# One store per output tile and buffer places taken in turn: a fused linear attention and channel mix on one core

## The chip, the cores and the metric

The kernel runs on one core of one Trainium2 chip. The metric is the time of one execution in microseconds (us) on the device, the median of several runs. A profiled execution gives a trace beside it; its span runs from the first to the last instruction.

## What is computed

The reference has two parts. For batch 8, 8 heads, 576 positions and head size 64, a linear attention:

```python
def phi(x):
    proj = np.einsum('bhsd,df->bhsf', x, w_phi)                 # 64 -> 128
    proj = proj - np.max(np.abs(proj), axis=-1, keepdims=True)
    return np.concatenate([np.exp(proj), np.exp(-proj)], axis=-1)
kv  = np.einsum('bhsf,bhsd->bhfd', phi(k), v)
num = np.einsum('bhsf,bhfd->bhsd', phi(q), kv)
den = np.einsum('bhsf,bhf->bhs', phi(q), phi(k).sum(2))[..., None] + 1e-06
```

The quotient num/den, its heads side by side, is the x of shape (8, 576, 512) of a channel mix, where x_prev is x moved on by one position:

```python
xk = mu_k * x + (1 - mu_k) * x_prev
xr = mu_r * x + (1 - mu_r) * x_prev
k  = np.maximum(xk @ w_k, 0)          # 512 -> 1024
v  = k * k @ w_v                      # 1024 -> 512
out = v / (1 + np.exp(-(xr @ w_r)))   # float32, (8, 576, 512)
```

## The kernel before

The whole program is unrolled. The work is cut into named operations, and the long string `ORDER` gives the order in which they are recorded; each engine executes its own part of that list in order. A name is followed, where it matters, by the engine (`/POOL`), the PSUM place (`:1`) and the number of matmuls that only fill time (`+1@0`). The framework derives the waits between engines from the tiles that an instruction reads and writes. An operation that is meant for the DMA (a name ending in `.d`) records nothing.

*Attention.* There are 32 head pairs, n = 4 x batch + a. Loads bring q and k of a batch to `nat` in bf16 (line 321, GpSimd's queue) and v to `vt` (line 327, SP's or GpSimd's). From batch 2 on, DMA transposes on SP's queue make `qkT` (`tr`, line 352). Each pair is projected (`kp`, `qp`, line 566), VectorE finds the largest magnitudes (`rk`, `rq`, lines 579 and 584), ScalarE takes exponentials (`ea`, `eb`, `qa`, `qb`, lines 605 and 643), TensorE forms `ps_kv` and `ps_nd` (`kv`, `nd`, lines 656 and 677), and VectorE divides into `x_sc` (`ra`, `rd`, lines 685 and 689).

*From attention to mix.* From pair 8 on, a DMA transpose on SP's queue (`xz`, line 700) turns x_sc into `xs`, positions along the free dimension. A small copy (`xu`, line 706) sets the shifted start, `df` (line 726) takes the difference to the position before, and `xa`, `xb` (line 732, VectorE) write `xk` and `xr` for two batches together.

*Channel mix.* A batch has four main tiles of 128 rows x 512, and each two batches share one edge tile of two 64-row halves. `h` (line 810) multiplies by w_k in eight blocks, `rl` (lines 206 and 208) is the relu into `krelu`, `sq` (lines 212 and 214) the square into `kk`; `r` (line 829) and `th` (line 835, tile `rt`) make the gate, `v` (line 843) multiplies by w_v, and `ob` (line 849, VectorE) combines gate and product into the output tile. `so` (line 856) stores it from SP's queue. The edge tile goes the same way (lines 897 to 942). A main tile holds, for two neighbouring values of s, 64 rows p of output position 9p + s, so a 64-row half lies in HBM in rows of 2 KB, 18 KB apart, and the other half begins 2 KB after it. A store is two DMAs of 64 rows, one for each half. The last edge tile is stored in quarters, three on SP's queue and one on ScalarE's.

*Buffers.* SBUF tiles come from pools. A tile name has a number of places (`BUFS`: 4 of `ob`, 3 of `krelu`, 3 of `rt`, 2 of `kk`, 2 of `nat` and so on), and the pool gives out one of them when `tile(...)` is called; the first writer of it waits for the readers of the tile that was there. `krelu`, `rt` and `ob` are called for in the matmul step ahead of the one that writes them:

```python
def vm(ci):
    def f():
        s["v", ci] = ps = motile(("mo", f"v{b}.{ci}"), "ps_v")
        s["o", ci] = mm.tile([128, DM], FP, name="ob", bufs=BUFS["ob"])
```

PSUM has two places "mo" of one bank for h, r, v and the small transposes, and three places "P" of two banks for the attention.

Of the kernel before, what the change touches and what calls it, by code (L numbers as in the profile page):

```python
# [126 lines left out]
so7.2 so7.2.d re3:0 ob7.3 so7.3 so7.3.d ve3.0:1 the3 ve3.1:0 obe3.0 soe3.0.a soe3.0.a.d obe3.1  # L127
soe3.0.b soe3.0.b.d soe3.1.b soe3.1.b.d soe3.1.a soe3.1.a.d
# [32 lines left out]
def kernel(  # L161
# [48 lines left out]
    def square(eng, out_, in_):  # L210
        if eng == "ACT":
            nc.scalar.activation(out_, in_, AF.Square)
        else:
# [4 lines left out]
            "xs": 2, "mhl": 3, "nmq": 3, "nmk": 3, "mT": 3, "kvs": 2, "x": 3, "me": 2, "d": 2, "mTe": 2}  # L218
# [81 lines left out]

    nat, qkT, vt = {}, {}, {}

    def get(dct, key, pool, shape, dtype, name, **kw):
        if key not in dct:
            dct[key] = pool.tile(shape, dtype, name=name, **kw)
        return dct[key]
# [5 lines left out]
    def add_load(b, a0, a1, at, first):  # L312
# [4 lines left out]
        def ld(which):  # L317
            def f():
                t = get(nat, b, inp, [128, NP, 2 * X], BF, "nat")
                src, o = ((k, 0), (q, X))[which]  # L320
                nc.gpsimd.dma_start(out=t[:, a0:a1, o:o + X], in_=heads(src, b, a0, a1))
            return f

        def ldv(c0, c1):
            def f(eng):
                t = get(vt, (b, c0 // 2), inp, [128, 2, X], FP, "vt", bufs=BUFS["vt"])
                (nc.sync if eng == "SP" else nc.gpsimd).dma_start(out=t[:, c0 % 2:c0 % 2 + c1 - c0, :],
                                                                  in_=heads(v, b, c0, c1))
            return f

        def pt(b, a, bk):
            def f():
                i = NP * b + a
                get(qkT, b, inp, [128, NP * R, 128], BF, "qkT")
                ps = motile(("mo", f"pt{i}.{bk}"), "ps_pt")
                st["pb", i, bk] = pb = ps.bitcast(BF).rearrange("p (g t) -> p g t", t=128)
                for g in range(5 * bk, min(R, 5 * bk + 5)):
                    nc.tensor.transpose(pb[:, g - 5 * bk, :], nat[b][:, a, g * 128:(g + 1) * 128], ident)
            return f
# [9 lines left out]
        def tr(p0, p1):  # L349
            def f():  # L350
                t = get(qkT, b, inp, [128, NP * R, 128], BF, "qkT")
                nc.sync.dma_start_transpose(out=t[:, R * p0:R * p1, :],
                                            in_=nat[b][:, p0:p1, :].rearrange("p a x -> p (a x)"))
            return f

        g = 0.95 * n
        if b == 0 and a0 == 0:
            def hk():
                st["kq"] = mm.tile([128, NFC, 512], BF, name="kk").rearrange("p a x -> p (a x)").bitcast(FP)[:, 0:2 * X].rearrange("p (i x) -> p i x", i=2)
                nc.sync.dma_start(out=st["kq"][:, 0, :], in_=heads(k, 0, 0, 1)[:, 0, :])  # L360
# [4 lines left out]
            def ck(i):  # L365
                def f(eng):
                    t = get(nat, b, inp, [128, NP, 2 * X], BF, "nat")
                    o = t[:, 0, i * X:(i + 1) * X]
                    copy(eng, o, st["kq"][:, i, :])
                return f  # L370
# [80 lines left out]
    def add_edge(b, a0, a1, first, it):  # L451
# [5 lines left out]
        def tp():  # L457
            s["ps"] = ps = ptile(A, "ps_e")
            for nm_, dct in (("tk0", tkp), ("tk1", tkn)):
                get(dct, b, mid, [128, NP, 128], BF, nm_)  # L460
# [9 lines left out]
        def rt_():  # L470
            s["m"] = m = small.tile([128, 2, NP], FP, name="me", bufs=BUFS["me"])
# [15 lines left out]
        def mce(eng):  # L487
            s["mT"] = small.tile([128, 128], BF, name="mTe", bufs=BUFS["mTe"])
# [57 lines left out]
    def add_pair(n):  # L546
# [30 lines left out]
        def rk():  # L577
            t = get(cp, "nmk", small, [128, 2, 8], FP, "nmk", bufs=BUFS["nmk"])
# [3 lines left out]
        def rq():  # L582
            t = get(cp, "nmq", small, [128, 2, 8], FP, "nmq", bufs=BUFS["nmq"])
# [18 lines left out]
        def ek(pn):  # L602
            def f():
                s[f"k{pn}"] = mid.tile([128, 8, 128], BF, name=f"k{pn}", bufs=BUFS["kpn"])
# [17 lines left out]
        def mc(eng):  # L622
            cp["mT"] = small.tile([128, 128], BF, name="mT", bufs=BUFS["mT"])
# [15 lines left out]
        def eq(pn):  # L639
            def f():  # L640

                t = s[f"q{pn}"] = mid.tile([128, 8, 128], BF, name=f"q{pn}", bufs=BUFS["qpn"])
# [22 lines left out]
        def kvc(eng):  # L665
            s["kv"] = small.tile([128, 2, 2, 65], BF, name="kv", bufs=BUFS["kvs"])
# [15 lines left out]
        def ra():  # L682
            s["rd"] = small.tile([128, 2, 5], FP, name="rden")
# [3 lines left out]
        def rd():  # L687
            s["x"] = mid.tile([128, 10, 64], BF, name="x_sc", bufs=BUFS["x"])
# [5 lines left out]
        def newx():  # L694
            for dct, nm_ in ((xkt, "xk"), (xrt, "xr")):
                get(dct, bp, mm, [128, NDC, 2 * S], BF, nm_)
# [27 lines left out]
        def df(eng):  # L724
            s["d"] = mid.tile([128, S], BF, name="diff", bufs=BUFS["d"])
# [69 lines left out]
    def add_moe(b):  # L795
# [4 lines left out]
        main = out[b].rearrange("(p s) d -> s p d", s=R)[b % 2:b % 2 + 8]  # L800
        mixa, mixb = ([f"x{i}{4 * b + a}" for a in range(NP)] for i in "ab")

        def h(fc):
            def f():
                s[fc] = ps = motile(("mo", f"h{b}.{fc}"), "ps_h")
                s["kr", fc] = mm.tile([128, 512], BF, name="krelu", bufs=BUFS["krelu"])
                if fc == 0:
                    s["kk"] = mm.tile([128, NFC, 512], BF, name="kk")
# [5 lines left out]
        def rl(fc):  # L814
            def f(eng):
                relu(eng, s["kr", fc], s[fc])
# [7 lines left out]
        def rr(ci):  # L824
            def f():
                s["r", ci] = ps = motile(("mo", f"r{b}.{ci}"), "ps_r")
                s["t", ci] = mm.tile([128, DM], BF, name="rt", bufs=BUFS["rt"])
# [5 lines left out]
        def th(ci):  # L833
            def f():
                nc.scalar.activation(s["t", ci], s["r", ci], AF.Tanh, scale=0.5)  # L835
            return f

        def vm(ci):
            def f():
                s["v", ci] = ps = motile(("mo", f"v{b}.{ci}"), "ps_v")  # L840
                s["o", ci] = mm.tile([128, DM], FP, name="ob", bufs=BUFS["ob"])
# [5 lines left out]
        def ob(ci):  # L847
            def f():
                nc.vector.scalar_tensor_tensor(out=s["o", ci], in0=s["t", ci], scalar=1.0,  # L849
# [3 lines left out]
        def so(ci):  # L853
            def f():
                for i in range(2):
                    nc.sync.dma_start(out=main[2 * ci + i], in_=s["o", ci][64 * i:64 * i + 64, :])
            return f

        for fc in range(NFC):
# [3 lines left out]
               alloc=[("mo", mo), ("krelu", ("krelu", nme))] + ([("kk", ("kk", b))] if fc == 0 else []),  # L863
               rel=[("xk", bp)] if fc == NFC - 1 else [])
            op("rl" + nme, "ACT", 0.6, ("rl",) + t, rl(fc), ["h" + nme], rel=[mo], alt=("ACT", "DVE"))
            op("sq" + nme, "POOL", 1.06, ("sq",) + t, sq(fc), alt=("POOL", "DVE", "ACT"), port=True, deps=["rl" + nme], rel=[("krelu", nme)])
        for ci in range(4):
# [3 lines left out]
               alloc=[("mo", mo), ("rt", ("rt", nme))], rel=[("xk", bp)])  # L871
            op("th" + nme, "ACT", 0.6, ("th",) + t, th(ci), ["r" + nme], rel=[mo])
# [3 lines left out]
               alloc=[("mo", mo), ("ob", ("ob", nme))], rel=[("kk", b)], chain="v")  # L876
            op("ob" + nme, "DVE", 0.7, ("ob",) + t, ob(ci), ["v" + nme, "th" + nme],
# [5 lines left out]
    def add_moe_edge(bp):  # L883
# [4 lines left out]
        def h(half):  # L888
            def f():
                s[half] = ps = motile(("mo", f"he{bp}.{half}"), "ps_he").rearrange("p (i t) -> p i t", i=4)  # L890
                s["kr", half] = mm.tile([128, 512], BF, name="krelu", bufs=BUFS["krelu"])
                if half == 0:
                    s["kk"] = mm.tile([128, NFC, 128], BF, name="kke", bufs=1)
# [9 lines left out]
        def rl(half):  # L903
            def f(eng):
                relu(eng, s["kr", half], s[half].rearrange("p i t -> p (i t)"))
# [7 lines left out]
        def rr():  # L913
            s["r"] = ps = motile(("mo", f"re{bp}"), "ps_re")
            s["t"] = mm.tile([128, DM], BF, name="rt", bufs=BUFS["rt"])
# [4 lines left out]
        def th():  # L920
            nc.scalar.activation(s["t"], s["r"], AF.Tanh, scale=0.5)

        def vm(c0, w):
            def f():
                s["v", c0] = ps = motile(("mo", f"ve{bp}" if w == DM else f"ve{bp}.{c0 // w}"), "ps_ve")
                if c0 == 0:
                    s["o"] = mm.tile([128, DM], FP, name="ob", bufs=BUFS["ob"])
# [5 lines left out]
        def ob(c0, w):  # L933
            def f():
                nc.vector.scalar_tensor_tensor(out=s["o"][:, c0:c0 + w], in0=s["t"][:, c0:c0 + w], scalar=1.0,
# [3 lines left out]
        def so(c0, w, which, e):  # L939
            def f():  # L940
                for i in ((0, 1) if which < 0 else (which,)):
                    (nc.scalar if e == "ACT" else nc.sync).dma_start(
                        out=out[b - 1 + i].rearrange("(p s) d -> s p d", s=R)[8 * (1 - i)][:, c0:c0 + w],
                        in_=s["o"][64 * i:64 * i + 64, c0:c0 + w])
            return f

        for half in range(2):
# [3 lines left out]
               alloc=[("mo", mo), ("krelu", ("krelu", nme))] + ([("kke", ("kke", bp))] if half == 0 else []))  # L951
            op("rl" + nme, "ACT", 0.6, ("rl",) + t, rl(half), ["h" + nme], rel=[mo], alt=("ACT", "DVE"))
# [3 lines left out]
        op("r" + nme, "PE", 0.87, ("un",) + t, rr, mixb + ["wr.d"], chain="r", alloc=[("mo", mo), ("rt", ("rt", nme))],  # L956
           rel=[("xk", bp)])
        op("th" + nme, "ACT", 0.6, ("th",) + t, th, ["r" + nme], rel=[mo])
        t = (4 * b, "ve")
        for hf in range(1 if bp < 3 else 2):  # L960
# [4 lines left out]
               alloc=[("mo", mo)] + ([("ob", ("ob", nme))] if hf == 0 else []), rel=[("kke", bp)], chain="v")  # L965
            op("ob" + nmv, "DVE", 0.7 * w / DM, ("ob",) + t, ob(hf * w, w), ["v" + nmv, "th" + nme],
               rel=[mo, ("rt", nme)])
            for i in ((-1,) if bp < 3 else (0, 1)):
                x = "so" + nmv + ("" if i < 0 else ".a" if i == 0 else ".b")
                e = "ACT" if hf == 1 and i == 1 else "SP"  # L970
                op(x, e, 1.2, ("so",) + t, so(hf * w, w, i, e), ["ob" + nmv])
                op(x + ".d", "DMA", 0.7, ("so",) + t, None, [x], rel=[("ob", nme)])

    BUFS["kke"] = 1
# [42 lines left out]
```

## Time and profile before

| | |
|---|---|
| time, median of 3 runs | 285.87 us |
| lowest and highest run | 284.57 and 334.05 us |
| profiled execution: span from first to last instruction | 275.3 us |
| profiled execution: own time | not given apart from the span; the median of the runs is 10.6 us above it |
| instructions in the trace | 8865 |
| bytes by DMA | 42.89 MB, 156 GB/s over the span |
| HBM read, written | 33.62 MB, 9.44 MB |
| TensorE clock granted | 1.00 |
| stores by SP's queue | 70 of 128 KB and 3 of 64 KB; one of 64 KB by ScalarE's |

Under "busy", PE is TensorE's matmuls and PEld its weight loads, DVE is VectorE, ACT ScalarE, POOL GpSimd and SP SyncE. Registers, semaphores and the issue of DMAs do not count as busy. The chain is followed back from the last instruction, at each step to what released it. The share of a DMA queue is the time of its packets over 16 engines and the span, and "to landing" is the time from the issue of a DMA to its completion.

### The profile page before, as it was taken

What the parts mean: (1) busy time and instruction counts of PE and PEld (TensorE: products, weight loads), DVE (VectorE), ACT (ScalarE), POOL (GpSimd) and SP (SyncE); (2) the same over time, 40 slices, a digit from 0 to 9 for tenths busy, and PEclk for the clock granted to TensorE, in tenths of its full rate; (3) what the DMA queues carried; (4) which work ended last, traced back from release to release, by engine and by line L of the source; (5) the groups of instructions that cost most, each with busy time, mean ns of one, the idle gap of its engine ahead of it and who ended that gap; (6) DMA issues with size and microseconds to landing.
All of it is one profiled execution on the core that took longest, in us unless ns stands there. A gap on an engine that the chain in (4) does not pass through costs nothing.

```text
span 275.3 us, 8865 instructions
## 1 busy us (share of the span) xinstructions
PE 261.7 (95%) x3682; PEld 154.1 (56%) x3730; DVE 234.6 (85%) x388; ACT 223.1 (81%) x413; POOL 142.4 (52%) x193
## 2 busy tenths in 40 slices
PE   7899889999899999999999999999999999999993
PEld 3567656566555566555565666555566565444542
DVE  6999999999799989999999889998889897864222
ACT  3899999999899997899898999789987777616330
POOL 5799557976818682633459465821931611300200
PEclk9999999999999999999999999999999999999999
DMA  7999999599999899759699998981725324142134
GB/s 147 285 209 250 209 213 174 114 235 175 238 129 200 202 219 185 155 127 248 99 166 164 215 249 142 171 255 41 161 89 88 77 52 100 42 110 67 29 88 116
DMA packets 65817, 42.89 MB, mean 156 GB/s; under 512 B 47152, under 2 KB 57008, under 8 KB 65776
## 3 DMA queue, kind: packets, MB, share of 16 engines
q1 hardware_dynamic: 54496, 27.54, 49.3%
q0 software_dynamic: 11056, 14.42, 29.1%
q8 instruction: 29, 0.48, 0.8%
q10 hardware_dynamic: 224, 0.36, 0.5%
q14 instruction: 12, 0.10, 0.1%
HBM read 33.62 MB, written 9.44 MB: 156 GB/s over the span
## 4 chain that ended last, share of the span: by engine, by line
PE 75%; DVE 8%; ACT 6%; issue 4%; DMA 3%; POOL 2%; SPq 0%; POOLq 0%; ACTq 0%
PE ps_h L810 19%; PE ps_v L843 17%; PE ps_r L829 9%; PE ps_nd L677 5%; PE ps_kv L656 5%; DMA qkT<-nat 3%; PE ps_he L897 3%; PE ps_ve L929 3%; PE ps_k L566 2%; PE ps_qT L630 2%; PE ps_q L566 2%; PE ps_qT L636 2%; ACT k L605 2%; DVE nmk L579 2%; PE ps_f L292 1%
## 5 line engine op out<-in xcount | busy, mean ns | idle before, releaser
L597 POOL TENSOR_TENSOR v<-vt,v 128x576 bf16<-128x576 f32 x59 | 69.8, 1203 | 33.5 <-ACT v L591 31.1
L605 ACT ACTIVATE k<-ps_k 128x1024 bf16<-128x1024 f32 x64 | 64.8, 1047 | 1.3 <-DVE nmk L579 1.3
L643 ACT ACTIVATE q<-ps_qT 128x1024 bf16<-128x1024 f32 x64 | 63.8, 1054 | 1.8 <-PE ps_qT L636 1.7
L810 PE MATMUL ps_h<-xk,wk_bf 128*128 128x512 bf16 x235 | 60.5, 380 | 1.2
L843 PE MATMUL ps_v<-wv_bf,kk 128*128 128x512 bf16 x244 | 58.2, 379 | 0.6
L579 DVE TENSOR_REDUCE nmk<-ps_k 128x8 f32<-128x1024 f32 x32 | 38.8, 1217 | 1.8 <-PE ps_k L566 1.5
L584 DVE TENSOR_REDUCE nmq<-ps_q 128x8 f32<-128x1024 f32 x32 | 38.3, 1217 | 1.6 <-PE ps_q L566 1.4
L843 PEld LDWEIGHTS <-kk 128*128 128x128 bf16 x256 | 24.1, 98 | 27.3
L810 PEld LDWEIGHTS <-wk_bf 128*128 128x128 bf16 x256 | 22.7, 97 | 25.0 <-issue 0.7
L206 ACT ACTIVATE krelu<-ps_h 128x512 bf16<-128x512 f32 x48 | 28.8, 611 | 9.3 <-PE ps_h L810 9.3
L726 POOL TENSOR_TENSOR diff<-xs 128x576 bf16<-128x576 bf16 x15 | 20.2, 1346 | 28.8 <-ACT xs L706 12.7
L214 POOL TENSOR_TENSOR kk<-krelu 128x512 bf16<-128x512 bf16 x18 | 19.1, 1068 | 30.3 <-ACT krelu L206 26.6
L849 DVE SCALAR_TENSOR_TENSOR ob<-rt,ps_v 128x512 f32<-128x512 bf16 x32 | 21.7, 682 | 14.3 <-PE ps_v L843 12.7
L829 PE MATMUL ps_r<-wr_bf,xr 128*128 128x512 bf16 x116 | 31.1, 380 | 0.7
L835 ACT ACTIVATE rt<-ps_r 128x512 bf16<-128x512 f32 x32 | 19.7, 615 | 8.8 <-PE ps_r L829 8.7
L732 DVE SCALAR_TENSOR_TENSOR xk<-diff,mu_k_t,xs 128x576 bf16<-128x576 bf16 x32 | 26.7, 839 | 0.1
L689 DVE TENSOR_TENSOR x_sc<-ps_nd,rden 128x640 bf16<-128x640 f32 x32 | 26.0, 817 | 0.6
L732 DVE SCALAR_TENSOR_TENSOR xr<-diff,mu_r_t,xs 128x576 bf16<-128x576 bf16 x32 | 25.6, 806 | 0.1
L656 PE MATMUL ps_kv<-v,k 64*128 64x65 bf16 x1024 | 22.4, 190 | 0.5 <-ACT q L643 0.2
L566 PEld LDWEIGHTS <-qkT 64*128 64x128 bf16 x512 | 16.5, 94 | 11.0 <-issue 8.0
L656 PEld LDWEIGHTS <-k 64*128 64x128 bf16 x1024 | 19.3, 94 | 5.7 <-issue 1.8
L677 PE MATMUL ps_nd<-kv,q 128*128 128x65 bf16 x512 | 21.4, 193 | 0.0
(102 smaller groups left out, 414.3 us busy)
## 6 DMA issues: line engine op xcount, KB each, us to landing
out_dram<-ob SPq DMA_DIRECT2D x70, 128.0 KB, 2.5
vt<-in_v_dram SPq DMA_DIRECT2D x11, 576.0 KB, 6.1
nat<-in_k_dram POOLq DMA_DIRECT2D x6, 576.0 KB, 7.8
nat<-in_q_dram POOLq DMA_DIRECT2D x6, 576.0 KB, 8.0
vt<-in_v_dram POOLq DMA_DIRECT2D x4, 576.0 KB, 6.0
wk_bf<-in_moe_w_k_dram POOLq DMA_DIRECT2D x2, 512.0 KB, 11.4
wv_bf<-in_moe_w_v_dram POOLq DMA_DIRECT2D x2, 512.0 KB, 10.6
nat<-in_k_dram POOLq DMA_DIRECT2D x3, 288.0 KB, 6.9
```

Source lines behind the costliest of these rows:

```text
L206: nc.scalar.activation(out_, in_, AF.Relu, scale=HALF)
L579: nc.vector.tensor_reduce(t[:, j, :], s["k"].rearrange("p a (g f) -> p (a g) f", f=128), axis=AX.X, op=ALU.max, apply_absolute_value=True, ...
L584: nc.vector.tensor_reduce(t[:, j, :], s["q"].rearrange("p a (g f) -> p (a g) f", f=128), axis=AX.X, op=ALU.max, apply_absolute_value=True, ...
L597: (nc.vector if eng == "DVE" else nc.gpsimd).tensor_tensor(vb[:, a, pn, :, 0:64], vt[b, a // 2][:, a % 2, :].rearrange("p (s d) -> p s d", ...
L605: nc.scalar.activation(s[f"k{pn}"], s["k"].rearrange("p a (g f) -> p (a g) f", f=128), AF.Exp, scale=(1.0 if pn == 0 else -1.0))
L643: nc.scalar.activation(t.rearrange("f x (a p) -> f x a p", a=2), s["qT"].rearrange("f a (x p) -> f x a p", p=64), AF.Exp, scale=(1.0 if pn ...
L656: nc.tensor.matmul(ps[:, hh, pn * 65:(pn + 1) * 65], lhsT=s[f"k{pn}"][r, c, :], rhs=vb[r, a, pn, 2 * g + par, :], start=(pn == 0 and c == ...
L677: nc.tensor.matmul(ps[:, bk, o * 65:(o + 1) * 65], lhsT=tail if sl < 2 else s[f"q{pn}"][:, 2 * G + h, :], rhs=s["kv"][:, h, pn, :], start= ...
L732: nc.vector.scalar_tensor_tensor(out=t[:, a, (b % 2) * S:(b % 2 + 1) * S], in0=s["d"], scalar=mu[:, a:a + 1], in1=xs[:, a, 0:S], op0=ALU.m ...
L810: nc.tensor.matmul(ps, lhsT=wk_bf[:, c, fc * 128:(fc + 1) * 128], rhs=xkt[bp][:, c, m0:m0 + 512], start=(c == 0), stop=(c == NDC - 1))
L829: nc.tensor.matmul(ps, lhsT=xrt[bp][:, c, m0 + ci * 128:m0 + (ci + 1) * 128], rhs=wr_bf[:, c, :], start=(c == 0), stop=(c == NDC - 1))
L843: nc.tensor.matmul(ps, lhsT=s["kk"][:, fc, ci * 128:(ci + 1) * 128], rhs=wv_bf[:, fc, :], start=(fc == 0), stop=(fc == NFC - 1))
```

## The change

*Stores.* Each output tile is stored by one DMA of 128 rows instead of two of 64. The destination is written as [2, 64, 512]: the two halves outermost, then 64 rows, then 512 numbers; for the edge tiles the same shape is put together from two addresses. The last edge tile is stored as two pieces of 256 columns, the first on SP's queue, the second on ScalarE's. The string `ORDER` changes in its last line alone.

```diff
         main = out[b].rearrange("(p s) d -> s p d", s=R)[b % 2:b % 2 + 8]
+        main = main.rearrange("(c i) p d -> c i p d", i=2)
...
         def so(ci):
             def f():
-                for i in range(2):
-                    nc.sync.dma_start(out=main[2 * ci + i], in_=s["o", ci][64 * i:64 * i + 64, :])
+                nc.sync.dma_start(out=main[ci], in_=s["o", ci])
             return f
...
-        def so(c0, w, which, e):
-            def f():
-                for i in ((0, 1) if which < 0 else (which,)):
-                    (nc.scalar if e == "ACT" else nc.sync).dma_start(
-                        out=out[b - 1 + i].rearrange("(p s) d -> s p d", s=R)[8 * (1 - i)][:, c0:c0 + w],
-                        in_=s["o"][64 * i:64 * i + 64, c0:c0 + w])
+        def so(c0, w, e):
+            def f():
+                rows = out[b - 1:b + 1].rearrange("i (p s) d -> i p s d", s=R)
+                lo, hi = rows[0, :, R - 1, c0:c0 + w], rows[1, :, 0, c0:c0 + w]
+                both = bass.AP(lo.tensor, lo.offset, [[hi.offset - lo.offset, 2]] + [list(x) for x in lo.ap])
+                (nc.scalar if e == "ACT" else nc.sync).dma_start(out=both, in_=s["o"][:, c0:c0 + w])
             return f
```

*Buffers.* Every place of every SBUF ring becomes a tile of its own with one place, and a counter takes the places in turn. The call moves from the matmul step to the step that writes the tile (`krelu` to `rl`, `rt` to `th`, `ob` to `ob`). The number of places of each ring stays.

```diff
+    used = {}
+
+    def slot(kind):
+        i = used[kind] = used.get(kind, -1) + 1
+        return i % BUFS[kind]
+
+    def ring(pool, kind, shape, dtype, name, i=None):
+
+        i = slot(kind) if i is None else i
+        return pool.tile(shape, dtype, name=name, tag=f"{name}.{i}", bufs=1)
+
...
         def vm(ci):
             def f():
                 s["v", ci] = ps = motile(("mo", f"v{b}.{ci}"), "ps_v")
-                s["o", ci] = mm.tile([128, DM], FP, name="ob", bufs=BUFS["ob"])
...
         def ob(ci):
             def f():
+                s["o", ci] = ring(mm, "ob", [128, DM], FP, "ob")
                 nc.vector.scalar_tensor_tensor(out=s["o", ci], in0=s["t", ci], scalar=1.0,
...
         def rl(fc):
             def f(eng):
+                s["kr", fc] = ring(mm, "krelu", [128, 512], BF, "krelu")
                 relu(eng, s["kr", fc], s[fc])
...
         def df(eng):
-            s["d"] = mid.tile([128, S], BF, name="diff", bufs=BUFS["d"])
+            s["d"] = ring(mid, "d", [128, S], BF, "diff")
```

The other tiles (`nat`, `qkT`, `vt`, `tk`, `me`, `mTe`, `nmk`, `nmq`, `k`, `q`, `mT`, `kv`, `rden`, `x_sc`, `xk`, `xr`, `kk`, `kke`) are edited as `diff` is.

## The prediction

> **What bounds the kernel now.** I read the busy table first, then the chain that ended last, then the DMA queues, because the change touches nothing but stores and buffers.
>
> ```profile
> PE 261.7 (95%) x3682; PEld 154.1 (56%) x3730; DVE 234.6 (85%) x388; ACT 223.1 (81%) x413; POOL 142.4 (52%) x193
> ...
> PE 75%; DVE 8%; ACT 6%; issue 4%; DMA 3%; POOL 2%; SPq 0%; POOLq 0%; ACTq 0%
> ```
>
> TensorE is busy 95% of the span and carries 75% of the chain. DMA has 3% of the chain and SyncE's queue 0%: neither the transfers nor their issue sets the end today. The DMA part and the list of issues:
>
> ```profile
> q1 hardware_dynamic: 54496, 27.54, 49.3%
> q0 software_dynamic: 11056, 14.42, 29.1%
> q8 instruction: 29, 0.48, 0.8%
> q10 hardware_dynamic: 224, 0.36, 0.5%
> ...
> out_dram<-ob SPq DMA_DIRECT2D x70, 128.0 KB, 2.5
> ...
> xs<-x_sc SPq DMA_TRANSPOSE x24, 3.2
> ```
>
> The shares are means over 16 engines. They add up to about 80%, so the engines are well loaded while they are loaded evenly. A half tile's store lands in 2.5 us, and the transposes of x_sc (line 700) go down the same SP queue. Two stretches of the trace say what stores meet (columns: stretch, its length, busy time of the five engines, TensorE clock, DMA share, GB/s):
>
> ```profile
> 70.00:239.00 169.00, 166.04 (x2430) 97.88 (x2462) 155.50 (x242) 147.60 (x267) 85.39 (x113) 1.00 0.79 152
> 239.00:275.30 36.30, 31.88 (x176) 15.88 (x176) 13.62 (x26) 11.63 (x22) 3.31 (x3) 1.00 0.37 85
> 266.60:271.80 5.20, 4.44 (x28) 2.53 (x26) 2.22 (x4) 0.60 (x1) 0.00 (x0) 1.00 0.66 151
> ```
>
> The first store is issued at 71 us, the last transpose at 237.9. The DMA view of the first stretch counts 50 half stores, that of the second 20 halves and four quarters. So the middle holds 25 tiles and the tail 11 in bytes. The third row has nothing but stores in flight. One more view, the DMA of 184.5 to 188.2 us, cut in 40 slices:
>
> ```profile
> DMA  9999999999999999998444211111000000100000
> GB/s 423 399 399 418 407 399 371 412 412 385 451 382 404 379 424 401 380 379 313 180 158 158 113 67 66 44 44 44 22 22 22 22 22 22 44 22 22 0 0 0
> ```
>
> Four half stores were issued from 180.9 on, and this is their burst: about 400 GB/s with all 16 engines full, 25 GB/s for one engine. In the third row above it is 151/(16 x 0.66) = 14.3 GB/s per busy engine. These are my two ends for what one engine does with 2 KB rows.
>
> **What the Trainium skill says.** Page "DMA: Bandwidth & Descriptors", section "Why a DMA increments its semaphore by 16 and not by 1": a copy runs on k engines, the largest k up to 16 that divides the slowest dimension above one of both access patterns, as the instruction carries them; on the hardware queues these are the lowest-numbered k, and each posts one completion. The trace of before agrees for even shapes: q10 carries one load of 128 rows and one store of 64 rows, and 224 - 192 leaves 32 completions, 16 for each. Section "Queues, rings and completion order": each engine consumes a queue's descriptors in ring order, and alternates between queues. No run here shows this by itself. Section "Rules for kernel authors" has two rules that pull apart here: use one 128-partition transfer instead of two halves, and keep a dimension below 16 from standing outermost.
>
> **The change, part by part.** *The store.* Before, a half is 64 rows to 64 rows: 16 engines, 4 rows each. After, the SBUF side is 128 rows, but the built instruction writes a destination of 2 x 64 x 512 (edge tiles too; the last two are 2 x 64 x 256). The slowest dimensions are 128 and 2, so k = 2: all 4608 output rows go through two engines. Per tile: 262,144 bytes / 2 / 25 GB/s = 5.24 us on each, at the low rate 9.17 us; before it was 0.66 to 1.15 us on each of sixteen. I take 5.24, since in the third row 16 engines read 64 rows at a time, and in the burst, with two halves in flight together, they were full speed; two engines alone have less reason to disturb each other.
>
> *What else these two engines carry.* 78.7% of the 169 us of the middle (q1 59.7, q0 18.1, instructions 0.9) is 133 us per engine. The 50 halves are 0.41 MB per engine, 16 to 29 us, so 104 to 117 us are loads and transposes. Part of it counts time twice, when two queues are in service (a stretch at 93 us shows a share of 1.10). At 25 GB/s their 19.2 MB would be 48 us per engine, too little for small packets. I take 90, ends 48 and 117.
>
> *Sum, middle.* 25 x 5.24 = 131, plus 90 = 221 us of work for two engines in 169 us: +52 (ends +10 and +79). So they become the bound. What waits: loads and transposes are spread over all engines and land with their slowest share, and in the SP queue they stand behind up to four stores (the ob ring), 21 us. In order, ob's VectorE instruction (line 849) waits for the store four tiles back; behind it stand the reductions of ps_k and ps_q, the x_sc products and the mixes, hence ScalarE's exponentials, and it holds one of the two "mo" PSUM places, hence TensorE. A late x_sc transpose stops xu, diff, mixes and then h and r.
>
> *Dry time.* While VectorE waits for a transpose that stood behind the stores, no new store is made, and the two engines can run dry afterwards. Before does not show it: from 0 to 50 us. I take 10% of 221, 22 us, because compute needs only 169 of the 221 and can refill the ring of four.
>
> *Tail.* 11 x 5.24 = 58 us, 1 us before the first and 2 us for the last to land, 61 in place of 36.3: +24. TensorE's 31.9 us lie inside.
>
> *Issue.* SP loses 37 of 73 stores' issues at 0.59 us, 22 us, worth nothing at a 0% share of the chain. At the very end ACT's store is the last issued, 0.4 us earlier than SP's last was.
>
> *Rings and waits.* TensorE, VectorE and GpSimd keep their order of instructions exactly. ob's 27 or so waits for two halves become waits for one, and VectorE loses 17 semaphore instructions of about 20 ns: 0.3 us. Some two dozen krelu, diff, me and kv writers wait for a neighbouring earlier reader, because places are taken in strict turn and at the writer instead of at the matmul. Each is within one operation (0.4 to 1.1 us), in either direction, and most are already satisfied: between -2 and +2 us, taken as 0.
>
> *Total.* 275.3 + 52 + 22 + 24 = 373 us of span. The profiled execution's own time is known only as this span; the median of 285.87 lies 10.6 above it, and I add that: 384 us.
>
> **The rivals.** *Sixteen engines all the same* (not slower): the engine count follows the SBUF side's 128 rows. Then both halves leave as one burst at the 25 GB/s seen, ob is free some 0.6 us earlier, the end comes 0.4 us earlier, and SP's queue has 22 us less. For it: the page's account of k is the only ground for two engines, and no DMA of before has a short outer dimension. Against: the built destination does. It decides if stores land in about 2.5 us. It gives 285 us; under 280 only if those 0.6 us reached the chain ten times, and VectorE waited for no store before.
>
> *Two engines at the low rate:* 14.3 GB/s. Middle 25 x 9.17 + 90 + 22 = 341 (+172), tail 101 + 3 (+68): 526 us. For it: the tail's stores ran so before, unloaded by others. Against: that was with 64 rows over 16 engines.
>
> *Two engines, but mostly hidden:* loads cost these engines 48 us, and the ring of four covers the middle; +10 and the tail's +24: 320 us. Against: 0.79 of DMA share in the middle.
>
> **How the numbers follow.** Two engines overloaded, 384: 0.82. Sixteen engines: 0.08. Low rate: 0.06. Hidden: 0.04. The likeliest one's own range is 320 (no dry time, loads at 48) to 439 (117 and 50 us dry); I go to 450 for a rate between the two ends. The rest, sixteen engines and the low rate, is 0.14, and a few hundredths of the main case lie outside. About 2% of the time is what a measurement of this kernel tells from no change: slower 0.91, same 0.07, faster 0.02.
>
> **What would show it.** The list of issues must have 35 stores of 256 KB, landing in 7 us alone and 10 to 20 us in the median; at k = 16 under 3. Completions tell k directly: q1 loses 64 rows to ACT's queue and 73 x 16 completions, and gains 36 x 2: 53,336 packets; at k = 16 it is 53,840. q10 then has 274 instead of 288. ob's line must wait for DMA of out_dram, the xu, diff or mix lines for DMA of xs, and TensorE's share must fall to about 70% with unchanged matmul durations. The mean DMA share must fall although two engines are full, since the bytes are the same in a longer span. If the stores land late and the span still stays under 310, the overload reasoning is wrong; if they land in 2.5 us, the engine count is.

## The result, and the profile after

The changed kernel takes 356.64 us (median of 6 runs, 354.22 to 362.11), the kernel before 284.74 us in the same comparison (6 runs, 278.77 to 334.05). The ratio is 1.277, with a 95% interval of 1.265 to 1.289; it leaves out the runs that a disturbance made longer, which the medians, above all that of the kernel before, still contain, so it lies above their quotient of 1.253. The profiled execution took 356.93 us and has a span of 355.1, so 1.8 us lie around the span. Every profiled execution of the experiments showed 1.7 to 1.9 as well.

Busy times, the clock, and the DMA in 40 slices, from the page of the kernel after:

```profile
PE 278.4 (78%) x3682; PEld 161.0 (45%) x3730; DVE 236.3 (67%) x388; ACT 224.2 (63%) x413; POOL 141.0 (40%) x193
...
PEclk9999999999986559999998998999986999999655
DMA  8999989997959849593999699893291893111111
GB/s 151 267 240 210 206 142 199 170 185 116 155 123 100 121 91 131 128 167 38 200 179 73 134 103 149 64 184 114 70 72 51 75 62 61 52 53 51 51 50 41
```

VectorE, ScalarE and GpSimd did the same work as before to within 2 us. The last six slices tell what the stores run at: 50 to 53 GB/s at a DMA share of one tenth (the last slice, in which they end, has 41). The number that the whole prediction hung on stands in the DMA part, together with the chain:

```profile
q1 hardware_dynamic: 53336, 27.47, 60.2%
q0 software_dynamic: 11056, 14.42, 23.6%
q8 instruction: 29, 0.48, 0.7%
q10 hardware_dynamic: 274, 0.43, 0.4%
...
PE 34%; DMA 28%; DVE 13%; issue 8%; POOL 6%; ACT 3%; SPq 1%; DVEq 0%; POOLq 0%; ACTq 0%
DMA xs<-x_sc 10%; PE ps_v L862 9%; DMA out_dram<-ob 9%; PE ps_h L829 8%; DMA vt<-in_v_dram 8%; PE ps_r L848 4%; PE ps_nd L694 3%; POOL v L610 3%; DVE nmq L597 2%; PE ps_kv L673 2%; DVE nmk L592 2%; DVE xk L751 1%; DVE x_sc L706 1%; DVE xr L751 1%; DMA wph_f<-in_w_phi_dram 1%
```

A completion is, as in the prediction, what an engine posts when its share of a DMA is done; it counts as a packet. 53,336 and 274 packets mean two completions for each store; sixteen would have given 53,840 and 288. DMA went from 3% to 28% of the chain and TensorE fell from 75% to 34%. The DMA part is made up of transposes of x_sc, stores and v loads. The waits, longest first (who waited, for what, us in total, times, longest):

```profile
POOL xs L201 <- DMA xs<-x_sc: 29.2, 6, 10.3
...
POOL v L610 <- DMA vt<-in_v_dram: 24.9, 4, 12.3
ACT xs L199 <- DMA xs<-x_sc: 24.3, 3, 17.4
...
DVE ob L869 <- DMA out_dram<-ob: 23.4, 8, 5.9
```

None of these was among the long waits before. Cut at the end of the last transpose's issue, now 294 us instead of 239, the two stretches of the prediction are these (columns as there):

```profile
70.00:294.00 224.00, 183.37 (x2438) 105.04 (x2472) 157.82 (x245) 150.55 (x270) 85.47 (x115) 0.90 0.98 115
294.00:355.10 61.10, 32.95 (x173) 16.34 (x174) 13.86 (x25) 11.12 (x21) 3.31 (x3) 0.81 0.17 51
```

The middle grew from 169 to 224 us, the tail from 36.3 to 61.1. In the slices in which nothing but stores run, two engines at 51 GB/s are 25.5 GB/s each. That no second pair helps can be counted in the trace's packet records: in the tail the 2 KB packets of the stores are in flight two at a time for 44.9 us, three for 4.5 us, and never more, although stores are queued behind each other.

### The profile page after: what moved, and what is told of

The parts are those of the page before. It is cut to its first block, busy times and chain, and to the rows that moved or that the text cites. A ratio compares the mean times of both kernels' runs of the same rounds, so it can differ in the third digit from the quotient of the medians.

```text
span 355.1 us, 8808 instructions
## 1 busy us (share of the span) xinstructions
PE 278.4 (78%) x3682; PEld 161.0 (45%) x3730; DVE 236.3 (67%) x388; ACT 224.2 (63%) x413; POOL 141.0 (40%) x193
## 3 DMA queue, kind: packets, MB, share of 16 engines
q1 hardware_dynamic: 53336, 27.47, 60.2%
q0 software_dynamic: 11056, 14.42, 23.6%
## 4 chain that ended last, share of the span: by engine, by line
PE 34%; DMA 28%; DVE 13%; issue 8%; POOL 6%; ACT 3%; SPq 1%; DVEq 0%; POOLq 0%; ACTq 0%
DMA xs<-x_sc 10%; PE ps_v L862 9%; DMA out_dram<-ob 9%; PE ps_h L829 8%; DMA vt<-in_v_dram 8%; PE ps_r L848 4%; PE ps_nd L694 3%; POOL v L610 3%; DVE nmq L597 2%; PE ps_kv L673 2%; DVE nmk L592 2%; DVE xk L751 1%; DVE x_sc L706 1%; DVE xr L751 1%; DMA wph_f<-in_w_phi_dram 1%
## 5 line engine op out<-in xcount | busy, mean ns | idle before, releaser
L610 POOL TENSOR_TENSOR v<-vt,v 128x576 bf16<-128x576 f32 x59 | 68.6, 1182 | 49.1 <-DMA vt<-in_v_dram 24.9
L862 PE MATMUL ps_v<-wv_bf,kk 128*128 128x512 bf16 x244 | 63.4, 403 | 7.8 <-POOL kk L213 3.7
L869 DVE SCALAR_TENSOR_TENSOR ob<-rt,ps_v 128x512 f32<-128x512 bf16 x32 | 21.8, 684 | 44.5 <-DMA out_dram<-ob 23.4
L862 PEld LDWEIGHTS <-kk 128*128 128x128 bf16 x256 | 25.3, 103 | 37.9 <-issue 9.2
L848 PE MATMUL ps_r<-wr_bf,xr 128*128 128x512 bf16 x116 | 34.4, 411 | 6.0 <-DVE ob L869 3.3
L205 ACT ACTIVATE krelu<-ps_h 128x512 bf16<-128x512 f32 x48 | 28.9, 609 | 12.9 <-PE ps_h L829 10.9
L673 PEld LDWEIGHTS <-k 64*128 64x128 bf16 x1024 | 19.9, 95 | 11.2 <-issue 5.7
L694 PE MATMUL ps_nd<-kv,q 128*128 128x65 bf16 x512 | 23.0, 200 | 0.0
```

The source lines that it names most:

```text
L610: (nc.vector if eng == "DVE" else nc.gpsimd).tensor_tensor(vb[:, a, pn, :, 0:64], vt[b, a // 2][:, a % 2, :].rearrange("p (s d) -> p s d", ...
L673: nc.tensor.matmul(ps[:, hh, pn * 65:(pn + 1) * 65], lhsT=s[f"k{pn}"][r, c, :], rhs=vb[r, a, pn, 2 * g + par, :], start=(pn == 0 and c == ...
L694: nc.tensor.matmul(ps[:, bk, o * 65:(o + 1) * 65], lhsT=tail if sl < 2 else s[f"q{pn}"][:, 2 * G + h, :], rhs=s["kv"][:, h, pn, :], start= ...
L848: nc.tensor.matmul(ps, lhsT=xrt[bp][:, c, m0 + ci * 128:m0 + (ci + 1) * 128], rhs=wr_bf[:, c, :], start=(c == 0), stop=(c == NDC - 1))
L862: nc.tensor.matmul(ps, lhsT=s["kk"][:, fc, ci * 128:(ci + 1) * 128], rhs=wv_bf[:, fc, :], start=(fc == 0), stop=(fc == NFC - 1))
```

## The experiments

All times are medians; "before" beside each is the kernel before on the same chip. Each version gives one profiled span as well, and what a version costs in us is read from spans, beside the 276.1 us of the rings alone.

**The two halves of the change, taken apart.** First the rings alone (the changed kernel, stores cut again):

```diff
-                nc.sync.dma_start(out=main[ci], in_=s["o", ci])
+                for i in range(2):
+                    nc.sync.dma_start(out=main[ci][i], in_=s["o", ci][64 * i:64 * i + 64, :])
```

(and the edge tiles in the same way).

> The changed kernel with every store as two DMAs of 64 rows again, so that only the rings are new. If the two engines of the merged store are the whole cause: 285 us, within 2% of before, half stores landing in about 2.5 us, no wait of ob for a store. If the strict turn of the buffer places has a part in the slowdown: clearly above 290 us, with the missing part up to 72 us in the other run.

Measured: 277.72 us, before 283.37, ratio 0.986 (0.976 to 0.995), span 276.1, half stores landing in 2.4 us. Then the opposite, the kernel before with the one-DMA stores of the change and its own pools:

> The kernel before with one DMA of 2 x 64 rows for each tile, its pools as they were. Two engines: 356 us, as the whole change, 53,336 packets on q1. If the rings had a part: less than the whole change by that part.

Measured: 357.78 us, before 283.37, ratio 1.272 (1.255 to 1.289), and 53,336 packets on q1. The stores are the whole loss. Whether the rings bring a gain was asked once more:

> The version with the new rings and stores in halves once more, in five rounds, beside the kernel before: the first time it was 1.4% faster with an interval that just left out no change. If the strict turn of the places gains: 0.98 to 0.99 again. If that was the scatter of the kernel before: an interval that takes in 1.

Measured: 277.85 us in 22 runs, before 283.13 in 28, ratio 0.997 (0.994 to 1.000). That takes in 1: no gain that this comparison shows. The runs of this version lie between 277.2 and 280.6 us, those of before between 277.0 and 290.6; that the narrower scatter comes from the rings is not shown.

**Does the loss add up as middle plus tail?** The stores before the last x_sc transpose as two halves, the later ones as one DMA, by a condition on the tile (for the edge tiles, `bp >= 2`):

```diff
+                if not (b >= 6 or (b, ci) == (5, 3)):
+                    for i in range(2):
+                        nc.sync.dma_start(out=main[ci][i], in_=s["o", ci][64 * i:64 * i + 64, :])
+                else:
+                    nc.sync.dma_start(out=main[ci], in_=s["o", ci])
```

> The changed kernel; only the stores after the last transpose of x_sc (11 tiles in bytes) are one DMA, the 25 before it are two halves. By the sum of the prediction only the tail grows, from 36 to 61 us: +24, ratio 1.08 to 1.09, with TensorE's share and clock unchanged until 239 us. If a single overloaded stretch were what slows everything: little here, under +10.

Measured: 303.38 us, ratio 1.075 (1.057 to 1.093), span 301.0. With the condition turned round:

> The other way round: the 25 tiles of the middle in one DMA, the last 11 tiles in two halves. If the parts add up: the last transpose of x_sc moves from 238 to about 292 us, and the tail is 36 us again: +54 to +58, ratio 1.19 to 1.20. If the backlog of the middle reaches into the tail: more than that, up to +72.

Measured: 335.66 us, ratio 1.190 (1.179 to 1.201), span 334.8. The stretches of the first and of the second, cut at the last transpose of each:

```profile
70.00:240.20 170.20, 168.25 (x2456) 99.30 (x2491) 157.41 (x246) 149.76 (x269) 87.06 (x115) 1.00 0.77 153
240.20:301.00 60.80, 32.90 (x175) 16.22 (x176) 13.40 (x26) 11.52 (x22) 3.31 (x3) 0.79 0.14 50
```

```profile
70.00:296.40 226.40, 181.60 (x2444) 104.65 (x2476) 157.99 (x246) 150.35 (x269) 85.53 (x115) 0.92 0.99 114
296.40:334.80 38.40, 31.90 (x175) 15.86 (x176) 14.10 (x26) 11.57 (x22) 3.31 (x3) 1.00 0.38 82
```

Over the span of the rings alone (276.1) they cost 24.9 and 58.7 us, together 83.6; the whole change costs 79.0. The parts add up to within 5 us, and the tail is 61 us wherever it is stored by one DMA, with 50 GB/s in it.

**Is it the number of engines, or the one large DMA?** Here main tiles take every second or every fourth column of the batch's 512, so that one DMA of 128 rows has an outermost destination dimension of 4 or 8. The same stride is used for the gate and for the product; edge tiles are stored as halves.

```diff
-        main = main.rearrange("(c i) p d -> c i p d", i=2)
+        main = [main[4 * (ci // 2):4 * (ci // 2 + 1)].rearrange("s (p u) d -> u s p d", u=2)[ci % 2] for ci in range(4)]
...
-                    nc.tensor.matmul(ps, lhsT=s["kk"][:, fc, ci * 128:(ci + 1) * 128],
+                    nc.tensor.matmul(ps, lhsT=s["kk"][:, fc, 256 * (ci // 2) + ci % 2:256 * (ci // 2 + 1):2],
```

> Main tiles take every second column, so that one DMA of 128 rows has a destination of 4 x 32 x 512; edge tiles as two halves. If the engine count follows the outer dimension: 4 engines, a store takes 2.6 us on each, middle 25 x 2.6 + 90 = 155 of 169 us, tail 29 of 36 us: nearly hidden, 280 to 295 us. If it is one DMA instead of two that costs: about 350 us. q1 must count 4 completions for each of the 32 main stores.

> The same with every fourth column: 8 x 16 x 512, 8 engines, 1.3 us on each. If the count follows the outer dimension: fully hidden, as with two halves, 277 to 285 us. If one DMA of 256 KB costs by itself: about 350 us.

Measured: 306.14 us for 4, 281.08 for 8, before 282.75 (277.71 to 288.12). The spans are 306.9 and 277.8 us, which is 30.8 and 1.7 more than with the rings alone. The DMA rows, first of 4, then of 8:

```profile
q1 hardware_dynamic: 53520, 27.47, 55.7%
```

```profile
q1 hardware_dynamic: 53648, 27.47, 50.1%
```

The rings alone had 54,416 packets. With 32 main stores, 54,416 - 32 x (32 - 4) = 53,520, and 54,416 - 32 x (32 - 8) = 53,648: each store has 4 or 8 completions where its two halves had 32. So one DMA of 256 KB is harmless when eight engines carry it; what costs is how few engines it gets. One large DMA and the stride in the matmuls together cost no more than the 1.7 us at 8. At 4 the expected 280 to 295 us were missed.

**Is a short outer dimension needed for it?** Plain rows, no third dimension, four DMAs for a tile:

```diff
-                nc.sync.dma_start(out=main[ci], in_=s["o", ci])
+                for i in range(2):
+                    for r0, r1 in ((0, 62), (62, 64)):
+                        nc.sync.dma_start(out=main[ci][i][r0:r1], in_=s["o", ci][64 * i + r0:64 * i + r1, :])
```

> No outer dimension at all: each half of a main tile is stored as 62 rows and 2 rows, plain shapes, four DMAs for a tile; edge tiles as halves. The largest number up to 16 that divides 62 is 2. If the count is by that rule: two engines again, 330 to 360 us (edge stores on 16 engines give a little back, twice as many issues on SP take a little). If only a short outer dimension is slow: 277 to 290 us.

Measured: 346.97 us, before 282.75. Its q1 has 53,648 packets: 64 pairs of DMAs with 2 + 2 completions in place of 16. The span of 345.5 us is 69.4 above the rings alone; 32 of the 36 tiles go through two engines, and 32/36 of the 79.0 us of the whole change are 70. So a tile costs as much in 62 rows as in 2 x 64, and 2 is the largest number up to 16 that divides 62. A short outer dimension is not needed.

**Capacity of the two engines, or the place behind the stores in one ring?** All stores on ScalarE's queue:

```diff
-                nc.sync.dma_start(out=main[ci], in_=s["o", ci])
+                nc.scalar.dma_start(out=main[ci], in_=s["o", ci])
```

> The changed kernel with all stores issued from ScalarE's queue, so that the x_sc transposes no longer stand behind stores in one ring; still 2 x 64 rows. If the capacity of the two engines is the bound, as the prediction has it: 345 to 370 us, perhaps more since ScalarE now waits for ob. If the place behind the stores in the ring is what costs: the middle's 54 us go to a good part, 305 to 325 us, and x_sc transposes land in about 3 to 6 us.

Measured: 362.24 us, before 282.75. Nothing came back on balance: the last x_sc transpose is issued at 296.8 us, in the changed kernel at 292.4. ScalarE's queue holds only 3% of this run's chain, some 11 us, so what its own waiting may have eaten seems far from the 55 us by which the middle had grown. As far as this run tells, the place in the ring is not the main cost; it is not a clean separation, since ScalarE now waits too (39.0 us for ps_h, 10.9 in the changed kernel). The waits for x_sc transposes fell from 57 to 23 us, and waits for transposes of q and k took their place:

```profile
POOL xs L201 <- DMA xs<-x_sc: 21.6, 3, 13.9
PEld L479 <- DMA qkT<-nat: 21.6, 3, 13.4
```

**Why four engines cost about 30 us.** (The 23 us in the expectation below is the difference of the two medians; the spans give 30.8.) The chain of that run, transfers alone (start, us, what):

```profile
96.19 23.32 DMA xs<-x_sc
...
169.65 15.51 DMA xs<-x_sc
```

The kernel before, cut finer than in the prediction (three of its stretches):

```profile
70.00:110.00 40.00, 38.31 (x653) 23.71 (x661) 37.35 (x58) 36.01 (x63) 24.25 (x36) 1.00 1.10 195
...
135.00:175.00 40.00, 39.52 (x630) 24.09 (x633) 37.34 (x55) 36.22 (x67) 27.85 (x31) 1.00 1.00 177
...
205.00:239.00 34.00, 33.74 (x445) 19.70 (x447) 30.35 (x53) 25.24 (x45) 8.82 (x11) 1.00 0.35 70
```

The middle is not one bucket. Until 110 us and again from 135 to 175 us the DMA share is 1.10 and 1.00, with 12 and 10 half stores in it, so the other transfers alone nearly fill the engines; late in the middle all of it together needs a third. Both long waits begin within these two stretches. So the first two batches were given their halves back, and four engines kept from batch 2 on:

> Four engines again, but the eight main tiles of the first two batches (stored up to about 130 us) go out as two halves with the columns of before. Why four engines cost 23 us although their work over the whole middle fits: if it is the stretch from 70 to 110 us, where the other transfers alone already fill the engines (share 1.10 before), the stall at 96 to 120 us goes and 288 to 296 us are left, with the second stall, at about 155 to 170 us, still there. If the cost of four engines lies evenly over all tiles: 300 us.

Measured: 288.92 us, before 283.13, ratio 1.032 (1.014 to 1.049). The span is 287.1, 19.8 us less than with all tiles at four engines and 11.0 more than with the rings alone: 8 of the 32 main tiles carried two thirds of the loss. In its chain the first wait for x_sc is gone and the second is left, 17 us earlier:

```profile
152.29 14.89 DMA xs<-x_sc
```

**Another issuer.** The same change on GpSimd's queue, `nc.gpsimd.dma_start` in both stores:

> The changed kernel with all stores issued from GpSimd's queue, the destination still 2 x 64 rows. If each store takes another pair of the 16 engines there, the load is even again: stores land in about 7 us, 280 to 300 us, with some loss because GpSimd now waits for ob and issues 37 stores. If it is the same pair each time: 350 us and more, and the DMA rate in the tail stays at 51 GB/s. If all 16 engines take part: 277 to 290 us and a landing under 4 us.

Measured: 336.69 us, ratio 1.199 (1.176 to 1.222). Stores landed in 11.1 us (8.7 at least), and GpSimd waited 19.9 us for ob:

```profile
out_dram<-ob POOLq DMA_DIRECT2D x35, 256.0 KB, 11.1
```

```profile
POOL out_dram L875 <- DVE ob L869: 19.9, 10, 5.8
```

None of the three expectations fits. In the page's slices of its tail the rate reaches 91 GB/s, above the 51 of one pair. The packet records say more: from 300 us on, four to six packets of the stores are in flight at once for 17 us and two for 3.5 us; between 70 and 240 us it is two for 57 us and four for 16 us. So the pair is not always the same one, but for most of the middle only one pair works at a time. How the remaining 56 us of span divide between engines and GpSimd's own waiting stays open.

No version that was run beats the kernel before by a margin that the comparison shows; the rings alone (0.997) equal it, and eight engines, 1.7 us of span behind the rings alone, come close.

## Why the prediction was right, point by point

*Engine count.* Right: the packet counts are those that were written down, to the packet, and 4, 8 and 62 rows follow the same rule. This is what the Trainium skill's page "DMA: Bandwidth & Descriptors", section "Why a DMA increments its semaphore by 16 and not by 1", states; these runs agree with it for outer dimensions of 2, 4 and 8 and for 62 rows.

*Rate.* Right: 25 GB/s per engine was taken from the burst before, 25.5 was measured where only stores run. The burst was not made of stores alone, as the prediction has it: its view moved 0.80 MB, and four half stores are 0.52. The rate held all the same. The low end of 14.3 did not come up in the tail.

*Tail.* 61 us predicted, 61.1 measured, and 60.8 in the run whose middle was as before, so no backlog of the middle is hidden in it.

*Middle.* 131 us of stores, 90 of other transfers and 22 dry were predicted, 243 us together; 224 were measured. The mis-sized terms are the last two: other transfers and dry time together are 224 - 131 = 93 us, not 112. The runs do not separate them; the packet records of the changed kernel show no store in flight for 64 us of the middle, in which the pair was dry or worked for the other transfers. The 90 had been picked between 48 and 117 and the 22 were a guess, so that the two missed by no more than 19 us is partly luck. That the sum came so close with 25 tiles in one bucket also owes something to the overload being large: at four engines the same sum (155 of 169 us) said "fits", and about 30 us were lost, mainly in two places where the other transfers were dense.

*From span to time.* Wrong: the 10.6 us between the span and the median of before do not lie around the execution. The profiled runs give 1.8 us, so the 275.3 us span stood for 277 us, among the quickest runs of before. Of the 27 us by which 384 exceeds 356.64, 9 are this and 18 the middle.

*Who waits.* Right for ob (23.4 us at line 869 and 4.4 at the edge tiles) and for xs (57 us on three engines). The v loads, 24.9 us, were covered only by "land with their slowest share".

*Rings, issue, waits of neighbours.* Costed at nothing. For the rings and the waits of neighbours the runs agree: 0.997 with an interval that takes in 1. The saved issues were not tried alone, and the last store issued is SP's (335.2 us), not ScalarE's (334.0) as predicted.

*Signs that were wrong.* TensorE's share fell to 78%, not 70. With its busy time of before it would be 74% of the shorter span; the rest is that its matmuls did not keep their durations: those of ps_v took 403 ns on average instead of 379, at a mean clock of 0.905. And the DMA share did not fall: the four queues of the page sum to 84.9% after 79.7% before, while the rate fell from 156 to 121 GB/s. In the tail the share is low: 0.17, and 0.12 from 335 us on, where only stores are left (two engines of sixteen are 0.125). In the middle, packets that are held up count as busy. The packet records show it for the transposes, whose packets have 256 bytes: in the middle their median is 18 ns in both kernels, but their mean rose from 28 to 72 ns, and one in a hundred took over 1.4 us. The landing times of stores, another sign, cannot be read: the views of the changed kernel give none.

## What to carry to other kernels

Before two transfers are made one, look at the outermost dimension of both access patterns in the built instruction: on SP's and ScalarE's queues the largest number up to 16 that divides both was the number of engines in every run here, and 62 rows are as bad as 2 x 64. Completions count it: the packets of a queue change by the number of DMAs times the number of engines. On GpSimd's queue this count did not tell: with the 37 stores it had 30,080 packets instead of 11,056, far more than their rows and two completions each. When a few engines carry more, add their work up stretch by stretch where the mean DMA share is high, since an average over the whole span hides both an overloaded pair and a crowded 40 us.

## What the runs showed of the hardware that was not expected

TensorE's granted clock halved around its waits. Before, it was 1.00 throughout. In a stretch of the changed kernel with TensorE nearly idle it is 0.50:

```profile
120.00:126.00 6.00, 1.05 (x20) 0.94 (x18) 1.81 (x5) 0.00 (x0) 0.00 (x0) 0.50 1.21 167
```

And it is still down when the wait is over. From 256.8 to 260.2 us TensorE is busy for 0.82 us, at a clock of 1.00; in the next 3.4 us it is busy for 3.37, at 0.51. From 325.0 to 328.5 us it is busy for 0.84 us at 1.00, and in the next 3.4 us for 3.10 at 0.50. So a stall costs slow matmuls after it as well: TensorE's busy time rose by 16.7 us for the same instructions.

The issue of a transpose grows too (nanoseconds, least, median, most; before, then after):

```profile
L700 SPq DMA_TRANSPOSE xs<-x_sc x24: 1200/1230/2597, 72.3 to 237.9; - x24
```

```profile
L719 SPq DMA_TRANSPOSE xs<-x_sc x24: 1201/3660/9052, 73.1 to 292.4; - x24
```

With four engines the median is 1354 ns, with eight 1286. With the stores on ScalarE's queue it is 1269 ns, as before, although the same two engines are just as full (the longest is still 7325 ns). So it is mainly the stores waiting in SP's own queue, not the full engines, that the longer issue goes with, and what stands behind it on SP becomes late too.
